# Split weights for the last eight column tiles of block 0 in a fused attention, feed-forward and expert kernel

## The chip, the cores and the metric

The kernel runs on one NeuronCore of a Trainium2 chip. The metric is the device time of one execution in microseconds (us). Three executions of the kernel before took 616.04, 618.12 and 615.83 us, median 616.04. The profile is of one execution that took 618.46 us; its traced span is 616.5 us, and 1.96 us lie around it.

## The reference

```python
scores = q @ k.T / sqrt(D)              # 2 batches, 8 heads, 768 positions, D = 64
keep   = (pos < 4) | (0 <= row - col < 128)   # 4 sink positions and a window of 128
a      = softmax(where(keep, scores, -1e9))
x      = (a @ v) as 1536 tokens x 512
h      = x @ w_in                       # 512 x 2048, given in float64
g      = maximum(0.01 * h, h)
x      = g @ w_out                      # 2048 x 512, given in float64
# then top-1 routing to 8 experts (512 -> 1024 -> 512, relu, capacity 384),
# each token's result times its gate probability
```

All results are float32. The two matrices of the first feed-forward network, `w_in` and `w_out`, arrive as float64 and are brought to float32 on the chip.

## The kernel before

The 1536 tokens are worked in six blocks of 256 (`j` = 0 to 5). For each block the first feed-forward network walks through its 2048 hidden columns in 16 tiles of 128 (`f`; `i` counts the iterations). For a tile, `FFN.first` (L841) multiplies the 512 inputs with the tile's columns of `w_in` into one PSUM bank `hps` of 128 x 256, `leak` applies the leaky ReLU, `split_g` splits the result in a high and a low part, and `second` (L887) multiplies it with the tile's rows of `w_out` and adds up into two PSUM banks `y`, 128 x 512 each. `second` runs `LAG` = 2 iterations behind `first`.

There are two ways to multiply. Blocks 1 to 5 use split operands: every float32 operand is the sum of a high part (rounded to float32r) and a low part (the rest, also float32r), and a product is three passes: high with high, high with low, low with high. The weights' parts are `wh` and `wl`, the inputs' `xth` and `xtl`, those of g the two halves of `gp`. Block 0 multiplies plain float32 operands, `cvt` (the converted weights) with `xth` (which holds float32 in block 0) and `gr`.

In block 0 the leaky ReLU is made of two ScalarE activations that both read `hps` (L852, L853) and a subtraction on GpSimd (L854). In the others it is a scaling on ScalarE (L857), a maximum on VectorE that reads `hps` and the scaled copy (L858), a cast on ScalarE (L867, high part) and a subtraction on GpSimd (L869, low part). While block 0 runs there is one bank for `hps`; later there are two.

Each tile's weights (512 KB as float64 in each matrix) are loaded by the SP queue, four tiles of buffers in all, and turned into float32 by VectorE: three instructions of 128 x 512 for each matrix (L779, L783, L789), so six for a tile. `convert()` runs four tiles ahead of `first` and is over with iteration 11 of block 0. `split` (L809, L810) makes `wh` by a cast on ScalarE and `wl` by a subtraction, on GpSimd in block 0 and on VectorE in block 1. A matrix of a tile is queued for splitting when its second product in block 0 is issued; one is split in each iteration of block 0 from the third on (14 of 32), two in each of block 1. Tiles 0, 1, 14 and 15 are also stored to a scratch in HBM (`wscr`, L814), since only 14 tiles' parts are kept, and reloaded later.

Between the steps of a block lie the steps of the attention for the tokens of the next block: 20 of them during block 0. An attention unit has, among others, `sps` (L501, scores), copies and predicated copies on ScalarE and VectorE (L506, L513), the maximum of a row `mx` (L514), exponentials (L219), the reciprocal of the sum `ri` (L226, L227), the scaling on GpSimd (L229), transposes, and the product with v (`ops`, L568).

Nearly all tiles of SBUF, converted weights, parts of weights, g, and the attention's keys, queries, values and transposed parts, come from one pool `c` of 70 buffers of 2 KB a partition. A buffer is given back after the last use of what it holds, and whoever asks for one when none is free waits.

The instructions of TensorE, ScalarE, GpSimd and of the SP queue keep the order in which the program is written. VectorE's order is made by a planner ahead of the run, by priority; the conversions in the loop over the blocks stand 100 behind (`BEHIND`). Every engine executes its queue in order. The clears of the result's buffers (`places<-zero`) are issued on the SP queue from iteration 8 on, two an iteration.

Of the kernel before, what the change touches and what calls it, by code (L numbers as in the profile page):

```python
# [8 lines left out]
F32 = mybir.dt.float32  # L9
F32R = mybir.dt.float32r  # L10
# [3 lines left out]
ALU = mybir.AluOpType  # L14
# [4 lines left out]
P = 128  # L19
# [19 lines left out]
LAG = 2  # L39
SPLIT = (1, 2)  # L40
CLEAR_AT, CLEAR = 8, 2
ROUTE = (2, 5, 9, 10, 11, 14)
HOLD, TAIL = 4, 1
QUIET = 2
# [676 lines left out]
class FFN:  # L721
# [12 lines left out]
    def __init__(self, nc, pools, A, xt, cap):  # L734
        self.nc, self.p, self.A = nc, pools, A
        self.xt, self.CAP = xt, cap
        self.DM, self.DFF = A["shape_in"]
        self.K = self.DM // P
        self.NF = self.DFF // P
        self.wide = A["w_wide"]  # L740
        self.w, self.v, self.raw, self.g, self.y = {}, {}, {}, {}, {}
        n = max(0, self.NF - self.CAP)
        self.saved = set(range(n)) | set(range(self.NF - n, self.NF))
        self.scr = self.p["dram"].tile([self.NF, 4, P, 512], F32, name="wscr") if n else None
# [58 lines left out]
    def split(self, f, x, eng):  # L803
# [8 lines left out]
        if f in self.saved:  # L812
            for a, t in enumerate((h, l)):
                nc.sync.dma_start(out=self.scr[f, 2 * x + a], in_=t.bitcast(F32))  # L814

    def reload(self, f):
        nc, c = self.nc, self.p["c"]
        self.w[f] = {}
        for x in range(2):
            t = [c.tile([P, 512], F32R, tag="c", name=nm) for nm in ("wh", "wl")]  # L820
            for a in range(2):
                nc.sync.dma_start(out=t[a].bitcast(F32), in_=self.scr[f, 2 * x + a])
            self.w[f][x] = t
# [5 lines left out]
    def first(self, j, f):  # L829
        nc, N = self.nc, self.N  # L830
        ps = self.p["psh"].tile([P, 512], F32, tag="h", name="hps")[:, 0:N]
        kc = lambda t: t.rearrange("p (k c) -> p k c", k=self.K)
        if j:
            wh, wl = map(kc, self.w[f][0])
            xh, xl = self.xt(j)
            mm = ((wh, xh), (wh, xl), (wl, xh))
        else:
            mm = ((kc(self.v[f][0]), self.xt(j)[0]),)
        mm = [(w[:, k, :], x[:, k, :]) for k in range(self.K) for w, x in mm]
        for n, (w, x) in enumerate(mm):  # L840
            nc.tensor.matmul(ps, lhsT=w, rhs=x, start=(n == 0), stop=(n == len(mm) - 1))  # L841
        self.g[j, f] = ps

    def leak(self, j, f):

        nc, N = self.nc, self.N
        ps = self.g[j, f]
        if j == 0:

            t = self.p["c"].tile([P, 2, N], F32, tag="c", name="gr")  # L850
            g, r = t[:, 0], t[:, 1]
            nc.scalar.activation(g, ps, AF.Relu)  # L852
            nc.scalar.activation(r, ps, AF.Relu, scale=-0.01)  # L853
            nc.gpsimd.tensor_tensor(out=g, in0=g, in1=r, op=ALU.subtract)  # L854
        else:
            g = self.p["g"].tile([P, N], F32, tag="g", name="g")
            nc.scalar.activation(g, ps, AF.Copy, scale=0.01)  # L857
            nc.vector.tensor_tensor(out=g, in0=ps, in1=g, op=ALU.max)  # L858
        self.g[j, f] = g

    def split_g(self, j, f, end=False):
        nc, N = self.nc, self.N
        g = self.g[j, f]
        if j == 0:
            return
        gp = self.p["c"].tile([P, 2, N], F32R, tag="c", name="gp")
        nc.scalar.copy(gp[:, 0], g)  # L867
        eng = nc.vector if end else nc.gpsimd
        eng.tensor_tensor(out=gp[:, 1], in0=g, in1=gp[:, 0].bitcast(F32), op=ALU.subtract)  # L869
        self.g[j, f] = gp  # L870

    def second(self, j, f, start, stop, tiles):
        nc = self.nc
        gp = self.g[j, f]
        if start:
            self.y[j] = [self.p["psy"].tile([P, self.DM], F32, tag=f"y{t}", name=f"y{t}")
                         for t in range(self.N // P)]
        for t in tiles:
            y = self.y[j][t]
            sl = slice(t * P, (t + 1) * P)  # L880
            if j:
                wh, wl = self.w[f][1]
                mm = ((gp[:, 0, sl], wh), (gp[:, 0, sl], wl), (gp[:, 1, sl], wh))
            else:
                mm = ((gp[:, sl], self.v[f][1]),)
            for n, (l, r) in enumerate(mm):
                nc.tensor.matmul(y, lhsT=l, rhs=r, start=(start and n == 0), stop=(stop and n == len(mm) - 1))  # L887
# [696 lines left out]
def build(tc, A, n_sink, window, capacity):  # L1584
    nc = tc.nc
# [3 lines left out]
    ring = RingAttention.fits(n_sink, window)  # L1589
# [9 lines left out]
    with ExitStack() as es:  # L1599
# [63 lines left out]
        ffn = FFN(nc, p, A, xt, FFN.CAP if ring else FFN.CAP - FEWER // 4)  # L1663
# [14 lines left out]
        def some(calls, n):  # L1678
            for f in calls[:n]:
                f()  # L1680
            del calls[:n]
# [19 lines left out]
        nclear = CLEAR * (ffn.NF - CLEAR_AT)  # L1701
        rate = -(-max(0, rt.NU * rt.E - nclear) // ROUTE[3])
        ex = Experts(nc, tc, p, A, rt, ident)
# [3 lines left out]
        pending, held, routing, splits = [], [], [], []  # L1707
# [7 lines left out]
        def split(n, f=-1, x=0):  # L1715

            while splits and (n > 0 or f >= 0 and x not in ffn.w.get(f, ())):
                ffn.split(*splits.pop(0), nc.vector if j else nc.gpsimd)
                n -= 1

        def second():
            j, f, i = pending.pop(0)
            if j == 1:
                split(0, f, 1)
            last = i == ffn.NF - 1
            if j == late and i >= ffn.NF - HOLD:

                ffn.second(j, f, i == 0, last, range(TPB - 1))
                held.append((j, f, i))
                if last:  # L1730
                    for t in range(TPB - 1):
                        rt.evac(j * TPB + t, ffn.y[j][t])
                return
            ffn.second(j, f, i == 0, last, range(TPB))
            del ffn.g[j, f]
            if j == 0:
                splits.extend((f, x) for x in range(2))
            elif i < n_ev or j == late:
                del ffn.w[f]
            if j > 1 and i < n_ev:  # L1740
                ffn.reload(ffn.order(j)[ffn.CAP + i])
            if last:
                ts = tuple(range(j * TPB, (j + 1) * TPB))
                for t, y in zip(ts, ffn.y.pop(j)):
                    rt.evac(t, y)
                routing.extend(route(ts))
                if j == late - 2 and rt.NU:
                    routing.insert(-1, ex.rank)

        for j in range(NB):  # L1750
# [9 lines left out]
            for i, f in enumerate(ffn.order(j)):  # L1760
# [18 lines left out]
                    step()  # L1779
                    ndone += 1  # L1780
                some(conv, 99)
                split(SPLIT[min(j, 1)])
                if j > 0 or i >= CLEAR_AT:
                    some(clears, max(1, rate) if j else CLEAR)
                if routing and i in ROUTE:
                    routing.pop(0)()
# [91 lines left out]
```

## Time and profile before

| | |
|---|---|
| median of three executions | 616.04 us (615.83 to 618.12) |
| profiled execution | 618.46 us, span 616.5 us |
| granted clock of TensorE | 0.984 of full speed in the mean |
| TensorE matmul busy | 586.6 us, 95% of the span, 3889 instructions |
| VectorE busy | 382.7 us, 62%, 928 instructions |
| ScalarE busy | 311.9 us, 51%, 920 instructions |
| GpSimd busy | 179.2 us, 29%, 328 instructions |
| moved by DMA | 91.88 MB, 149 GB/s in the mean |

Block 0 lasts from about 37 to 122 us, blocks 1 to 5 to about 431 us; the experts follow. A busy share is an average over all of these. In a row PE is TensorE, PEld its weight load, DVE VectorE, ACT ScalarE, POOL GpSimd and SP the queue that issues most DMAs. `L841` is line 841 of the kernel; `out<-in` names the tiles written and read. A time in brackets is idle time ahead of an instruction and what ended it. The chain of waits follows the last instruction back through whatever released it, so it tells at every time which engine the end hangs on.

### The profile page before, as it was taken

The page shows a single profiled execution, that of the slowest core. Times are in us where ns is not written, and L with a number is a line of the kernel's source. Part 1 is how long each engine was busy: PE and PEld are TensorE (multiplying, and loading weights), DVE is VectorE, ACT ScalarE, POOL GpSimd, SP SyncE. Part 2 cuts the span into 40 slices and gives each one's busy share as a digit, 9 for nine tenths or more (in the row PEclk, how much of TensorE's full clock was granted, in tenths as well). Part 3 has the DMA queues.
Part 4 walks back from the last instruction along what each step waited for, and adds up shares of the span by engine and source line. Part 5 has one row for each costly group of instructions (what it writes and reads, how often), then busy time and mean ns, then how long its engine had stood idle before and what let it go on. Part 6 is the DMA issues. An engine that isn't in the chain of part 4 may idle for free.

```text
span 616.5 us, 11665 instructions
## 1 busy us (share of the span) xinstructions
PE 586.6 (95%) x3889; PEld 502.4 (81%) x3889; DVE 382.7 (62%) x928; ACT 311.9 (51%) x920; POOL 179.2 (29%) x328
## 2 busy tenths in 40 slices
PE   7698998999999999999999999999999999999994
PEld 7575665689889888998889988988798989998783
DVE  4789998377854555555655542266456676655992
ACT  4665555576655455545555433254244544444772
POOL 4425555633342224332422232223110120102110
PEclk9899999999999999999999999999969999999998
DMA  9769989622653402330223015755165856643950
GB/s 244 185 206 249 294 231 269 158 83 53 226 185 108 115 19 69 87 103 19 61 58 98 1 48 164 259 183 165 59 207 172 259 177 204 195 133 111 304 188 12
DMA packets 83564, 91.88 MB, mean 149 GB/s; under 512 B 42964, under 2 KB 51156, under 8 KB 83473
## 3 DMA queue, kind: packets, MB, share of 16 engines
q1 hardware_dynamic: 81488, 85.68, 47.1%
q0 software_dynamic: 1984, 5.13, 2.3%
q8 instruction: 39, 0.64, 0.4%
q14 instruction: 53, 0.43, 0.2%
HBM read 72.01 MB, written 20.09 MB: 149 GB/s over the span
## 4 chain that ended last, share of the span: by engine, by line
PE 70%; DVE 13%; DMA 7%; issue 7%; ACT 3%; POOL 0%; another core or an unknown queue 0%; POOLq 0%; SPq 0%; ACTq 0%; DVEq 0%
PE y L887 18%; PE hps L841 17%; PE ph L1306 10%; PE py L1355 8%; PE ops L568 4%; DVE cvt L789 3%; PE sps L501 3%; DMA out<-ys,gt 2%; DVE word L779 2%; DVE word L783 2%; DMA craw<-in_moe_w 2%; PE lps L972 2%; PE sps L652 1%; PE pps L536 1%; PE kps L163 1%
## 5 line engine op out<-in xcount | busy, mean ns | idle before, releaser
L887 PE MATMUL y<-wh,gp 128*128 128x512 f32 x320 | 115.9, 403 | 0.7 <-ACT gp L867 0.7
L869 POOL TENSOR_TENSOR gp<-g,gp 128x256 fp32r<-128x256 f32 x77 | 56.8, 738 | 197.3 <-ACT gp L867 172.3
L841 PE MATMUL hps<-xth,wh 128*128 128x256 f32 x320 | 92.8, 290 | 0.0
L841 PE MATMUL hps<-xtl,wh 128*128 128x256 f32 x320 | 90.1, 281 | 0.0
L841 PE MATMUL hps<-xth,wl 128*128 128x256 f32 x320 | 89.9, 281 | 0.0
L1170 DVE TENSOR_TENSOR cw<-craw,cw 128x512 fp32r<-128x512 f32 x128 | 83.4, 695 | 9.1 <-ACT cw L1168 7.9
L1168 ACT CAST cw<-craw 128x512 fp32r<-128x512 f32 x112 | 63.4, 621 | 23.7 <-PE py L1355 22.3
L887 PEld LDWEIGHTS y<-wh,gp 128*128 128x128 f32 x320 | 60.0, 188 | 14.3 <-issue 2.7
L857 ACT ACTIVATE g<-hps 128x256 f32<-128x256 f32 x80 | 30.6, 382 | 70.0 <-PE hps L841 65.7
L1355 PE MATMUL py<-cw,ht 128*128 128x512 f32 x264 | 63.9, 397 | 0.2 <-DVE ht L1343 0.2
L841 PEld LDWEIGHTS hps<-xth,wh 128*128 128x128 f32 x320 | 60.3, 188 | 3.3 <-issue 0.9
L841 PEld LDWEIGHTS hps<-xtl,wh 128*128 128x128 f32 x320 | 60.3, 188 | 3.1 <-issue 0.7
L887 PE MATMUL y<-wl,gp 128*128 128x512 f32 x160 | 62.7, 392 | 0.0
L1306 PE MATMUL ph<-xt,cw 128*128 128x256 f32 (+2 forms) x444 | 62.3, 304 | 0.4 <-issue 0.4
L1306 PEld LDWEIGHTS ph<-xt,cw 128*128 128x128 f32 x444 | 61.1, 204 | 0.7 <-issue 0.5
L841 PEld LDWEIGHTS hps<-xth,wl 128*128 128x128 f32 x320 | 60.6, 189 | 0.0
L1355 PEld LDWEIGHTS py<-cw,ht 128*128 128x128 f32 x264 | 49.1, 189 | 11.5 <-DVE ht L1343 0.7
L858 DVE TENSOR_TENSOR g<-hps,g 128x256 f32<-128x256 f32 x80 | 33.4, 418 | 25.6 <-ACT g L857 25.3
L219 ACT ACTIVATE pm<-pm,mx 128x132 f32<-128x132 f32 (+1 forms) x80 | 31.7, 398 | 29.1 <-DVE mx L514 28.9
L867 ACT CAST gp<-g 128x256 fp32r<-128x256 f32 x80 | 33.3, 416 | 23.8 <-DVE g L858 23.6
L1364 POOL DMA_INDIRECT out<-ys,gt x11 | 11.4, 1036 | 114.7 <-DVE ys L1363 114.7
L543 DVE TENSOR_TENSOR pt<-pps,both 128x512 f32<-128x512 f32 x28 | 19.3, 688 | 35.7 <-PE pps L538 35.7
(211 smaller groups left out, 1121.0 us busy)
## 6 DMA issues: line engine op xcount, KB each, us to landing
craw<-in_moe_w SPq DMA_DIRECT2D x128, 256.0 KB, 3.5
rawi<-in_moe_w_in SPq DMA_DIRECT2D x16, 512.0 KB, 5.0
rawo<-in_moe_w_out SPq DMA_DIRECT2D x16, 512.0 KB, 5.4
places<-zero SPq DMA_DIRECT2D x24, 257.0 KB, 5.7
wh<-wscr SPq DMA_DIRECT2D x16, 256.0 KB, 2.9
wl<-wscr SPq DMA_DIRECT2D x16, 256.0 KB, 3.4
xg<-places SPq DMA_DIRECT2D x12, 257.0 KB, 4.4
natv<-in_v SPq DMA_DIRECT2D x12, 256.0 KB, 5.2
```

The costliest lines, as they stand in the source:

```text
L219: nc.scalar.activation(pm[:, e, 0:w], pm[:, e, 0:w], AF.Exp, bias=mx[:, e:e + 1], accum_out=su[:, e:e + 1])
L568: nc.tensor.matmul(ps[64 * e:64 * e + 64, :], lhsT=l, rhs=r, start=(x == 0), stop=(x == len(mm[0]) - 1))
L841: nc.tensor.matmul(ps, lhsT=w, rhs=x, start=(n == 0), stop=(n == len(mm) - 1))
L857: nc.scalar.activation(g, ps, AF.Copy, scale=0.01)
L858: nc.vector.tensor_tensor(out=g, in0=ps, in1=g, op=ALU.max)
L867: nc.scalar.copy(gp[:, 0], g)
L869: eng.tensor_tensor(out=gp[:, 1], in0=g, in1=gp[:, 0].bitcast(F32), op=ALU.subtract)
L887: nc.tensor.matmul(y, lhsT=l, rhs=r, start=(start and n == 0), stop=(stop and n == len(mm) - 1))
L1168: nc.scalar.copy(h, t)
L1170: eng.tensor_tensor(out=l, in0=t, in1=h.bitcast(F32), op=ALU.subtract)
L1306: nc.tensor.matmul(self.ph[f][:, sl], lhsT=self.w[e, "a", h, k][w][:, f * P:(f + 1) * P], rhs=self.xt[:, a, k, sl], start=(m == 0), stop=( ...
L1355: nc.tensor.matmul(self.py[n], lhsT=x, rhs=w, start=(h == 0 and f == 0 and m == 0), stop=(h == self.NH - 1 and f == self.HF - 1 and m == 2))
```

## The change

The products of the last eight column tiles of block 0 (f = 8 to 15) use split operands, as the blocks after it do. For this the inputs of block 0 are split once, in iteration 5 (`split_x0`: two casts on ScalarE and two subtractions on GpSimd, 128 x 512, into four buffers of the pool `c`). In iterations 6 to 13 both matrices of the tile two ahead are split on GpSimd in place of the one from the queue; these tiles go the way of the later blocks in `leak`, `split_g` and `second`, and aren't queued for splitting any more. The rule for the second way is `in_parts`, asked in `first`, `leak`, `split_g` and `second` (the line with `if j == 0:` below stands so in both `leak` and `split_g`). In the remaining iterations the queue is served as before, so 6 of the first eight tiles' 16 matrices are split in block 0 and 10 in block 1.

```diff
+AHEAD = 8
...
+    def split_x0(self):
+        nc, c = self.nc, self.p["c"]
+        for k in range(0, self.K, 2):
+            x = self.xt(0)[0][:, k:k + 2, :]
+            h, l = (c.tile([P, 2, self.N], F32R, tag="c", name=nm) for nm in ("x0h", "x0l"))
+            nc.scalar.copy(h, x)
+            nc.gpsimd.tensor_tensor(out=l, in0=x, in1=h.bitcast(F32), op=ALU.subtract)
+            self.x0.append((h, l))
+
+    def in_parts(self, j, f):
+        return j > 0 or f in self.ahead
...
-        if j:
+        if self.in_parts(j, f):
             wh, wl = map(kc, self.w[f][0])
-            xh, xl = self.xt(j)
+            xh, xl = [[x[:, k, :] for k in range(self.K)] for x in self.xt(j)] if j else \
+                [[self.x0[k // 2][a][:, k % 2, :] for k in range(self.K)] for a in range(2)]
             mm = ((wh, xh), (wh, xl), (wl, xh))
...
-        if j == 0:
+        if not self.in_parts(j, f):
...
-            if j:
+            if self.in_parts(j, f):
...
-                splits.extend((f, x) for x in range(2))
+                splits.extend((f, x) for x in range(0 if f in ffn.ahead else 2))
...
-                split(SPLIT[min(j, 1)])
+                if j == 0 and ring and i == AHEAD - 3:
+                    ffn.split_x0()
+                if j == 0 and ring and AHEAD <= i + 2 < ffn.NF:
+                    ffn.ahead.add(i + 2)
+                    for x in range(2):
+                        ffn.split(i + 2, x, nc.gpsimd)
+                else:
+                    split(SPLIT[min(j, 1)])
```

## Rows read from the trace of the kernel before

**Rows 1.** The page's chain that ended last, shares of the span by line.
```profile
PE y L887 18%; PE hps L841 17%; PE ph L1306 10%; PE py L1355 8%; PE ops L568 4%; DVE cvt L789 3%; PE sps L501 3%; DMA out<-ys,gt 2%; DVE word L779 2%; DVE word L783 2%; DMA craw<-in_moe_w 2%; PE lps L972 2%; PE sps L652 1%; PE pps L536 1%; PE kps L163 1%
```
**Rows 2.** Busy by stretch (us): stretch, length, PE, PEld, DVE, ACT, POOL, clock, DMA.
```profile
85.50:107.00 21.50, 19.48 (x106) 13.51 (x107) 18.45 (x41) 13.30 (x45) 10.62 (x16) 1.00 1.04 259
107.00:122.00 15.00, 15.00 (x80) 9.84 (x79) 6.43 (x17) 9.09 (x30) 9.22 (x15) 1.00 0.71 174
122.00:134.00 12.00, 12.00 (x78) 9.32 (x77) 6.87 (x17) 7.23 (x22) 5.12 (x9) 1.00 0.36 110
```
**Rows 3.** The chain in order of time: start us, us, what.
```profile
107.03 1.72 PE y L887 x4
...
108.75 1.73 PE hps L841 x8
...
113.20 1.73 PE hps L841 x8
...
122.58 1.43 PE hps L841 x12
...
132.91 1.39 PE y L887 x6
```
**Rows 4.** Timeline of VectorE, 74 to 124 us: start us, us, instruction, [idle before].
```profile
101.41 0.49 DVE L513 COPY_PREDICATED pm<-sel,sps 128x128 f32<-128x128 int32 x2
...
103.83 0.17 DVE L226 TENSOR_SCALAR ri<-su 128x2 f32<-128x2 f32 x1 [1.01 <-ACT pm L219]
...
106.37 0.69 DVE L789 SCALAR_TENSOR_TENSOR cvt<-rawo,word 128x512 int32<-128x512 int32 x1
```
**Rows 5.** Timeline of TensorE, 78 to 108 us.
```profile
78.65 1.89 PE L841 MATMUL hps<-xth,cvt 128*128 128x256 f32 x8
...
98.42 1.88 PE L887 MATMUL y<-cvt,gr 128*128 128x512 f32 x4
...
101.75 0.54 PE L197 MATMUL qps<-ident_r,qs 128*128 128x128 f32 x4 [0.18 <-DVE pm L513]
...
102.13 1.96 PE L841 MATMUL hps<-xth,cvt 128*128 128x256 f32 x8
...
106.40 0.64 PE L501 MATMUL sps<-kT,qT 128*128 128x264 f32 x3 [1.04 <-DVE qT L202]
```
**Rows 6.** Groups by line and shape: xcount | busy us, mean ns | idle before.
```profile
L857 ACT ACTIVATE g<-hps 128x256 f32<-128x256 f32 x80 | 30.6, 382 | 70.0 <-PE hps L841 65.7 <-PE y L887 1.8 <-PE pps L538 1.5
...
L858 DVE TENSOR_TENSOR g<-hps,g 128x256 f32<-128x256 f32 x80 | 33.4, 418 | 25.6 <-ACT g L857 25.3
...
L854 POOL TENSOR_TENSOR gr<-gr 128x256 f32<-128x256 f32 x16 | 11.9, 743 | 14.3 <-ACT gr L853 14.2
...
L810 POOL TENSOR_TENSOR wl<-cvt,wh 128x512 fp32r<-128x512 f32 x14 | 18.4, 1314 | 28.9 <-ACT wh L809 28.9
...
L809 ACT CAST wh<-cvt 128x512 fp32r<-128x512 f32 x32 | 19.5, 641 | 0.0
```
**Rows 7.** Waits between 78 and 107 us: in total, times, longest.
```profile
ACT pm L219 <- DVE mx L514: 8.6, 3, 4.5
```
**Rows 8.** Timeline of GpSimd, 60 to 135 us.
```profile
78.00 1.45 POOL L810 TENSOR_TENSOR wl<-cvt,wh 128x512 fp32r<-128x512 f32 x1
```
**Rows 9.** Timeline of VectorE, the operation ri.
```profile
78.25 1.23 DVE L226 TENSOR_SCALAR ri<-su 128x2 f32<-128x2 f32 x1
...
87.62 0.17 DVE L226 TENSOR_SCALAR ri<-su 128x2 f32<-128x2 f32 x1 [1.01 <-ACT pm L219]
```
**Rows 10.** Timeline of the SP queue.
```profile
103.78 0.39 SPq L140 DMA_DIRECT2D natk<-in_k  x1
...
121.74 0.39 SPq L140 DMA_DIRECT2D natv<-in_v  x1
```
**Rows 11.** Timeline of ScalarE, 122 to 136 us.
```profile
126.93 0.43 ACT L149 CAST ks<-natk 128x256 fp32r<-128x256 f32 x1
```
**Rows 12.** Waits of the SP queue, 96 to 150 us.
```profile
SPq L140 <- PE y L887: 19.0, 1, 19.0
```

More of the change, by code (lines that the diff above doesn't have):

```diff
@@ L741, in __init__ @@
         self.w, self.v, self.raw, self.g, self.y = {}, {}, {}, {}, {}
+        self.ahead, self.x0 = set(), []
         n = max(0, self.NF - self.CAP)
@@ L832, in first @@
         kc = lambda t: t.rearrange("p (k c) -> p k c", k=self.K)
-        if j:
+        if self.in_parts(j, f):
             wh, wl = map(kc, self.w[f][0])
-            xh, xl = self.xt(j)
+            xh, xl = [[x[:, k, :] for k in range(self.K)] for x in self.xt(j)] if j else \
+                [[self.x0[k // 2][a][:, k % 2, :] for k in range(self.K)] for a in range(2)]
             mm = ((wh, xh), (wh, xl), (wl, xh))
         else:
-            mm = ((kc(self.v[f][0]), self.xt(j)[0]),)
-        mm = [(w[:, k, :], x[:, k, :]) for k in range(self.K) for w, x in mm]
+            x = self.xt(j)[0]
+            mm = ((kc(self.v[f][0]), [x[:, k, :] for k in range(self.K)]),)
+        mm = [(w[:, k, :], x[k]) for k in range(self.K) for w, x in mm]
         for n, (w, x) in enumerate(mm):
@@ L863, in split_g @@
         g = self.g[j, f]
-        if j == 0:
+        if not self.in_parts(j, f):
             return
```

## The prediction

> **What bounds the kernel now.** I read the page's busy shares and chain first, then the chain in order of time through block 0, then the engines' busy time by stretch, then each engine's timeline where the chain changes hands.
>
> TensorE's products of the first feed-forward network, L887 and L841, head the chain that ended last; of VectorE's lines there the conversion of the weights has three (L789, L779, L783, 3 + 2 + 2%) [rows 1]. That conversion happens only up to the end of block 0, so the question is which engine carries block 0 when its last eight tiles run. The stretches answer it [rows 2]. Between 85.5 and 107 us VectorE is busy 18.45 of 21.50 us and TensorE 19.48; between 107 and 134 us TensorE is busy 27.00 of 27.00 and VectorE 13.30. In order of time the chain is VectorE's conversions and the attention work between them, then softmax and copies on ScalarE and two copies of qT on VectorE, and from 106.4 TensorE alone, product after product without a break [rows 3]. VectorE's timeline shows the hand-over: two predicated copies at 101.41 stand behind a conversion, and the last conversion begins at 106.37 [rows 4]. TensorE's timeline agrees: it waits for those copies at 101.75 (0.18 us) and last for VectorE's qT at 106.40 (1.04 us) [rows 5].
>
> Tiles 8 to 12, five, have their first product from 78.65 to 102.13, and the second product of tile 9, the latest ahead of the hand-over, is at 98.42 [rows 5]. So tiles 8 to 12 with their first product, and 8 and 9 with their second, run while VectorE is the bound. The first products of tiles 13 to 15 and the second ones of 10 to 15 lie in TensorE's own stretch.
>
> **The change part by part.**
>
> *The products.* In block 0 a first product is eight records in 1.73 us and a second one four in 1.72; in block 1, with split operands, they are twelve in 1.43 and six in 1.39 [rows 3]. A tile saves 0.30 + 0.33 = 0.63 us. Behind 107 us that is 3 x 0.30 + 6 x 0.33 = 2.9 us, all on the path, since TensorE has no gap there. Ahead of 107 us it is 5 x 0.30 + 2 x 0.33 = 2.2 us, which I count as nothing: TensorE would reach the copies at 101.41 sooner and wait. Its bounds are 0 and -2.2.
> [...]
>
> *The leaky ReLU of the eight tiles.* Before, two ScalarE reads of the product (0.38 each, as the scaling's) and a GpSimd subtraction (0.74); after, one ScalarE scaling (0.38), a VectorE maximum (0.418), a ScalarE cast of the same size and a GpSimd subtraction of the same shape [rows 6]. ScalarE and GpSimd come out even. VectorE gains 0.418 us a tile. Tiles 8 to 11 come ahead of its last conversion: 4 x 0.418 = 1.67 us on the bound; the other four lie where VectorE is half idle and cost nothing. Bounds: 0, if they fall into gaps such as that of 1.01 us at 103.83 [rows 4]; and 1.67 + 4 x 0.32 = 2.9, if each maximum also holds VectorE up until ScalarE's scaling is done, as the 25.6 us of idle time over 80 of them say [rows 6]. I take 1.67.
> There is one bank for the first product in block 0, so the next first product waits for the last reader. That was ScalarE's second read; now it is VectorE's maximum, behind at most one conversion (0.68 to 0.70, as the one at 106.37 [rows 4]): 0.38 + 0.70 + 0.42 = 1.50 us after the product. A second product (1.39) and mostly attention stand between: at most 0.1 us a tile. Nothing.
>
> *The weights split two tiles ahead.* Eight more splits move from VectorE in block 1 to GpSimd in block 0, a second one in each of the iterations 6 to 13. ScalarE casts earlier, not more in all: eight times 0.64 us, and two more casts for x; it is busy 13.30 of 21.50 and 9.09 of 15.00 us [rows 2, 6], and its own waits for VectorE's maxima of the scores (8.6 us between 78 and 107) cover it [rows 7]. Without that cover it is up to 10 x 0.64 = 6.4 us; I take 0. GpSimd takes ten more subtractions of 1.31 us [rows 6]. Until 107 it has room, 10.62 of 21.50 us busy. From 107 to 122 it is busy 9.22 of 15.00 [rows 2], 2.7 us of each interval of 4.4 (108.75 to 113.20 [rows 3]); with a second subtraction that is 4.0 against 4.4 - 0.6 = 3.8. In iterations 12 and 13 it falls behind by 0.2 us each, and two tiles of lead hold that. 0; the other end is both subtractions in full, 2.6. Block 1 gives nothing back: TensorE is busy all of 122 to 134 us, so 5.5 us less of VectorE there (8 x 0.69, its size in block 1 by estimate from the 0.68 to 0.70 of a conversion of the same shape [rows 4]) is off the path.
>
> *GpSimd against VectorE.* The tiny scaling ri (128x2) takes 0.17 us alone at 87.62, and 1.23 us at 78.25, just behind the start of a wl at 78.00 on GpSimd [rows 8, 9]. A hit costs 1.06 us, and until 107 on the bound. There are four ri from 78 to 107 us, one an attention unit. With two subtractions in a row instead of one I take one hit more, 1.06 us. Bounds: 0 and three more, 3.2. The maximum itself is not held up so: its mean over 80 is 418 ns [rows 6], beside GpSimd's subtractions of g.
>
> *Queues and space.* The scratch stores of tiles 14 and 15 (eight of 256 KB) come forward from block 1 to iterations 12 and 13. Behind them on the SP queue wait the clears, which nothing needs soon, and the keys issued at 103.78 [rows 10] with their queries; ScalarE takes those keys at 126.93 [rows 11]. Issued after the split of tile 15 (about 112 to 115 us by the intervals above), they have over 10 us to land. 0; the other end is a tile's interval, 4.4. The pool of 70 buffers holds, by the code, 14 x 2 + 18 = 46 weights at the end of block 0 now and 22 x 2 + 10 = 54 then, plus four for x until tile 15. The load of v issued at 121.74 already waits for a buffer that a second product frees, 19.0 us [rows 10, 12]. Extra waits there are free; on ScalarE's queue one would not be (below).
>
> *Sum:* -2.9 + 1.67 + 1.06 = -0.2 us. The profiled execution took 618.46 us (616.5 of span); so 618.3 for it, and on the median of 616.04, **615.9 us**. No change that can be told: what TensorE saves behind 107 us is about what VectorE loses ahead of it.
>
> **The rivals.**
> 1. *VectorE's additions find gaps and TensorE keeps everything.* For it: TensorE is busy 19.48 of the 21.50 us from 85.5 [rows 2], so it is nearly a bound itself, and VectorE has 3 us idle between 85.5 and 107. Against: the chain there runs through VectorE without a break, and its order is fixed before the run. 8 x 0.63 = 5.0: 611.0 us.
> 2. *GpSimd holds VectorE off (slower).* Place: ri and the small operations of attention on VectorE, iterations 6 to 11; price 1.06 each. -2.9 + 1.67 + 1.06n passes +3.1 from n = 5 on: 620.1. For it: ri is hit already with half the subtractions [rows 8, 9]. Against: the maxima and the conversions, most of the work there, show no such lengths [rows 4, 6].
> [...]
> 3. *ScalarE waits for a buffer (slower).* With 54 + 4 weights and x, three of g and a dozen of attention the pool is full from iteration 13 to block 1's second. ScalarE is in order; a cast that waits for a second product to free its buffer waits up to a tile's interval, 4.4 us. Against: blocks 1 and later run full without such a wait. -0.2 + 4.4: 620.2.
> 4. *The saving doesn't arrive,* since TensorE waits for GpSimd's wl or low part of g: the 2.6 us above, 618.5.
>
> **How the numbers follow.** 0.5% is 3.1 us, about what a measurement of this kernel can tell from no change. The forecast with its own range (613.0 to 618.2: one end with the maxima and hits free, the other with the larger price of the maxima and two hits): 0.52. Rival 1: 0.20. Rivals 2 and 3: 0.10 each. Rival 4: 0.08. Faster: rival 1 and a little of the forecast, 0.23; slower: rivals 2 and 3, 0.20; same 0.57. The range reaches from 611.5, near rival 1, to 620.0, near rivals 2 and 3.
>
> **What would show it.** Right: first products of tiles 8 to 15 as twelve records in about 1.43 us; eight more wl on GpSimd (22 in all), ten on VectorE; VectorE's last conversion about 2.7 us later than 107.1; TensorE's gaps ahead of it grown by 4 to 5 us; behind it no gap; block 1's first product at about 121.8 instead of 122.0, and everything after it shifted by that. Wrong: the last conversion at 107 or before (rival 1); ri above 1 us five times or more (rival 2); ScalarE's or TensorE's idle time near 115 to 130 us ended by a release of a buffer (rival 3); weight loads of the first product that wait for wl (rival 4).

## The result: slower by 3.4 us

The changed kernel took 619.99 us in the median (618.10 to 621.34), the kernel before beside it 616.58 (615.83 to 618.12): ratio 1.0054, 95% interval 1.0038 to 1.0069. Forecast were 615.9 us and no change that can be told; the range reached to 620.0. Run again in a later batch, the same code took 622.78 against 617.49 (1.0100, 1.0076 to 1.0123). Times of one kernel spread by 2 to 9 us from execution to execution (two that took more than twice as long, 1492.67 us of the maximum alone and 1434.94 of a kernel before, are in no ratio). A profile is of one execution: that of after took 620.08 us (span 618.3, mean granted clock 0.987), that of before 618.46 (616.5, 0.984). The latter is longer than each of the eight that its median of 616.58 comes from, so the two profiles lie closer together than the medians.

All 17 profiles of this study (the two given ones, one of after again, 14 of variants) can be cut into the same stages: what lies ahead of block 0's first product, block 0 from there to the first transposition `xps` of its result (some 12 us into block 1), blocks 1 to 5 up to the last `xps`, and the experts behind. The first stage takes 35.7 to 37.0 us (52.9 in one variant), blocks 1 to 5 take 298.2 to 298.7 us in every profile. So a loss of several us lies in block 0 or behind block 5. In the two profiles of after, block 0 took 98.56 and 97.58, and 97.09 in that of before; behind block 5 it is 184.3 and 184.4 against 183.9.

Inside block 0 the terms are not those of the prediction. By stretches after (length, TensorE, its weight loads, VectorE, ScalarE, GpSimd, clock, DMA), to be set against [rows 2]:
```profile
85.50:107.00 21.50, 17.62 (x133) 13.97 (x133) 18.50 (x42) 12.98 (x42) 13.43 (x19) 1.00 0.86 231
107.00:122.00 15.00, 12.45 (x90) 10.13 (x91) 8.42 (x20) 11.23 (x35) 12.91 (x17) 1.00 0.54 195
```
GpSimd went from 10.62 and 9.22 us to 13.43 and 12.91. TensorE idles 3.9 us in the first stretch and 2.6 in the second, where it idled 2.0 and not at all; VectorE is as full as before in the first stretch and fuller in the second. TensorE's timeline (start, us, instruction, idle time before it and its releaser) names the new waits:
```profile
77.08 0.80 PE L569 MATMUL ops<-pt,natv 128*64 128x128 f32 x8 [1.88 <-POOL pt L551]
...
98.53 0.38 PE L858 MATMUL hps<-x0h,wh 128*128 128x256 f32 x1 [2.55 <-DVE g L875]
```
The product with v (`ops`) waits five times, 5.1 us in all, for masks that GpSimd lays over `pt` (L551), and the first product of tile 11 waits once for VectorE's maximum that frees the single bank. None of them is in the kernel before. GpSimd's timeline ahead of the first one:
```profile
71.64 2.51 POOL L825 TENSOR_TENSOR x0l<-xth,x0h 128x512 fp32r<-128x512 f32 x2 [6.53 <-ACT x0h L824]
74.10 1.29 POOL L812 TENSOR_TENSOR wl<-cvt,wh 128x512 fp32r<-128x512 f32 x1
75.33 0.65 POOL L230 TENSOR_TENSOR pm<-pm,ri 128x264 f32<-128x264 f32 x1
75.92 0.75 POOL L871 TENSOR_TENSOR gr<-gr 128x256 f32<-128x256 f32 x1
76.60 0.79 POOL L551 TENSOR_SCALAR_AFFINE_SELECT pt<-pt 128x256 f32<-128x256 f32 x2
```
GpSimd stands idle for 6.53 us, then has 5 us of work ahead of the mask. It waits for ScalarE's cast of x, which stands in ScalarE's timeline behind exponentials that wait for VectorE's row maximum:
```profile
68.55 0.41 ACT L220 ACTIVATE pm<-pm,mx 128x132 f32<-128x132 f32 x1 [4.52 <-DVE mx L515]
...
70.92 1.16 ACT L824 CAST x0h<-xth 128x512 fp32r<-128x512 f32 x2
```
The split is written behind the iteration's second attention step, so two in-order queues pass that wait on.

### The profile page after: what moved, and what is told of

Read it like the earlier page. It is cut to its first block, busy times and chain, and to the rows that moved or that the text cites. A ratio compares the mean times of both kernels' runs of the same rounds, so it can differ in the third digit from the quotient of the medians.

```text
span 618.3 us, 11785 instructions
## 1 busy us (share of the span) xinstructions
PE 579.5 (94%) x3937; PEld 501.1 (81%) x3937; DVE 383.2 (62%) x928; ACT 314.3 (51%) x922; POOL 189.4 (31%) x338
## 5 line engine op out<-in xcount | busy, mean ns | idle before, releaser
L904 PE MATMUL y<-wh,gp 128*128 128x512 f32 x352 | 127.6, 403 | 0.7 <-ACT gp L884 0.7
L886 POOL TENSOR_TENSOR gp<-g,gp 128x256 fp32r<-128x256 f32 x85 | 63.4, 746 | 198.5 <-ACT gp L884 172.5
L904 PEld LDWEIGHTS y<-wh,gp 128*128 128x128 f32 x352 | 66.1, 188 | 15.8 <-issue 3.3
L874 ACT ACTIVATE g<-hps 128x256 f32<-128x256 f32 x88 | 33.6, 382 | 76.2 <-PE hps L858 75.6
L904 PE MATMUL y<-wl,gp 128*128 128x512 f32 x176 | 69.0, 392 | 0.0
L1323 PE MATMUL ph<-xt,cw 128*128 128x256 f32 (+2 forms) x444 | 59.2, 295 | 1.1 <-DVE xt L1311 1.1
L1323 PEld LDWEIGHTS ph<-xt,cw 128*128 128x128 f32 x444 | 58.0, 194 | 1.4 <-DVE xt L1311 1.3
L875 DVE TENSOR_TENSOR g<-hps,g 128x256 f32<-128x256 f32 x88 | 36.8, 418 | 28.4 <-ACT g L874 28.1
L884 ACT CAST gp<-g 128x256 fp32r<-128x256 f32 x88 | 36.6, 416 | 31.1 <-DVE g L875 29.8
```

The costliest lines, as they stand in the source:

```text
L1323: nc.tensor.matmul(self.ph[f][:, sl], lhsT=self.w[e, "a", h, k][w][:, f * P:(f + 1) * P], rhs=self.xt[:, a, k, sl], start=(m == 0), stop=( ...
```

## Experiments on block 0

**Load alone.** The kernel before with ten subtractions more on GpSimd, which read what was long there:
```diff
+        def load(t):
+            spare = p["c"].tile([P, 2, N], F32, tag="c", name="spare")
+            nc.gpsimd.tensor_tensor(out=spare, in0=t, in1=t, op=ALU.subtract)
...
+                if j == 0 and i == AHEAD - 3:
+                    for k in range(0, ffn.K, 2):
+                        load(xt(0)[0][:, k:k + 2, :])
+                if j == 0 and AHEAD <= i + 2 < ffn.NF:
+                    load(ffn.v[i + 2][0].rearrange("p (k c) -> p k c", k=2))
```


> The kernel before, with ten more GpSimd subtractions of 128x512 at the places where the change puts its ten (two in iteration 5 on the inputs, one in each of iterations 6 to 13 on weights); their results are used by nothing. Measure: time from block 0's first product to the first transpose of its result (97.1 us before, 98.6 after the change) and the total. Theory G (GpSimd's queue holds up the masks pt that TensorE's ops wait for, and the small operations of VectorE): TensorE waits for pt 3 to 5 us in all, block 0 is 2 to 4 us longer, total +2 to +4 us. Theory V (VectorE's maximum holds the only bank of the first product): no change, within 0.5 us in block 0, total within 1 us.


617.29 us, ratio 0.9989 (0.9974 to 1.0004); block 0 97.92, as in other kernels with an unchanged block 0 (below), and one wait of `ops` for a mask, 0.63 us. GpSimd's load by itself costs nothing that shows.

**The maximum alone.** Tiles 8 to 15 of the kernel before with the scaling, VectorE's maximum from the bank and one addition of zero on GpSimd:
```diff
+            if f >= AHEAD:
+                nc.scalar.activation(r, ps, AF.Copy, scale=0.01)
+                nc.vector.tensor_tensor(out=r, in0=ps, in1=r, op=ALU.max)
...
+                nc.gpsimd.tensor_tensor(out=g, in0=r, in1=self.zero, op=ALU.add)
```


> The kernel before, plain products, but tiles 8 to 15 of block 0 make g by a ScalarE scaling, a VectorE maximum that reads the bank, and one GpSimd addition of zero in place of the subtraction (same shape, so GpSimd's load stays). Theory V: TensorE waits for the maximum about 2.5 us around tile 11, VectorE's last conversion is 1.7 us or more later, block 0 is 1.5 to 3 us longer, total +1.5 to +3 us. Theory G: no wait above 0.5 us, block 0 within 0.7 us of 97.1, total within 1 us.


619.89 us, 1.0028 (1.0009 to 1.0046); block 0 98.15. Neither theory has it: the total is near theory V's, but the bank didn't hold TensorE. At 84.19 `ops` waited 3.08 us for GpSimd's masks, which stood behind the addition that waited for a late maximum.

**The bank freed by ScalarE.** The changed kernel with two activations of ScalarE in block 0 and VectorE's subtraction in SBUF:
```diff
+            if j == 0:
...
+                nc.scalar.activation(g, ps, AF.Relu)
+                nc.scalar.activation(r, ps, AF.Relu, scale=-0.01)
+                nc.vector.tensor_tensor(out=g, in0=g, in1=r, op=ALU.subtract)
```


> The changed kernel, but the bank is read by ScalarE alone: two activations as in the kernel before, then a VectorE subtraction of the two in SBUF in place of the maximum. Theory V: the wait of 2.55 us ahead of tile 11's first product goes, block 0 falls from 98.6 to about 96.2 us, total -2.4 against the changed kernel, so about +1 against the kernel before. Theory G: another wait takes its place, above all for pt; block 0 stays within 0.7 us of 98.6, total +2.5 to +4.


624.76 us, 1.0105 (1.0070 to 1.0140); block 0 102.33. The wait of 2.55 us is gone, but the waits for masks grow to 3.87 and 2.83 us. The maximum as the cause of the loss falls.

**The splits sooner.** The changed kernel with the casts and subtractions ahead of the second attention step:
```diff
+                if early_split(j, i):
+                    if i == AHEAD - 3:
+                        ffn.split_x0()
...
                 while more():
                     step()
...
-                if j == 0 and ring and i == AHEAD - 3:
-                    ffn.split_x0()
```


> The changed kernel, but the splits of the tile two ahead (and of the inputs) stand ahead of an iteration's second attention step instead of behind it, so ScalarE casts and GpSimd subtracts while ScalarE would wait for VectorE's row maxima. Theory G: TensorE's waits for pt (5.1 us in five gaps) fall below 2 us, block 0 falls from 98.6 to 95 to 97 us, total -1.5 to -3.5 against the changed kernel, so about 0 against the kernel before. Theory V: the wait for the maximum stays at about 2.5 us and block 0 within 0.7 us of 98.6.


Block 0 95.35, as expected, and one wait for a mask is left (0.83 us at 98.41). So the order of the queues was what cost there. But the whole took 619.18 us, 1.0024 (1.0002 to 1.0046): the stage behind block 5 was 190.1 us long where it is 183.9 in the profile of before. A stage that no edit had touched was 6 us longer, in a profile whose execution is the longest of the twelve (622.69 us).

## Experiments behind block 5

**Four runs to see whether that is chance, a shift, or code.** The changed kernel again; sooner splits with the leak of block 0 as before (`if j == 0:` in `leak`); the kernel before with 40 short products in place of 10 at its start; and with the last tile's first products of block 0 computed twice:
```diff
-WARM = 10
+WARM = 40
...
-            nc.tensor.matmul(warm, lhsT=ident, rhs=ident, start=True, stop=True)
+            nc.tensor.matmul(warm[:, 0:16], lhsT=ident, rhs=ident[:, 0:16], start=True, stop=True)
...
+        for again in range(2 if j == 0 and f == 15 else 1):
```


> The changed kernel once more, beside the others of this batch, for a second trace of it. Theory Q (GpSimd's in-order queue: masks stand behind subtractions that wait for ScalarE's casts) expects block 0 (first hps to first xps) at 98.3 to 98.8 us again, with five waits of TensorE's ops for the masks that sum to 4.5 to 5.5 us. On the whole time 1.003 to 1.007 of before.


Block 0 97.58, shorter than expected, and the same five waits; 622.78 us, 1.0100, a larger loss than expected.


> The changed kernel with the splits ahead of the second attention step, and in block 0 the leak as before (two activations of ScalarE, a subtraction of GpSimd) instead of VectorE's maximum. Theory Q and the experiment with sooner splits leave in block 0: one wait of 0.3 us for the maximum and the work of eight maxima on VectorE. If VectorE's maxima cost only themselves (1.67 us of its work), block 0 comes to 94.0 to 95.3 us, 0 to 1.3 under the 95.35 of sooner splits. Rival: GpSimd, which then has eight subtractions more (3.2 us), is the queue that fills, and waits of ops for masks come back: block 0 at 96 to 97.5. Whole time by the first 614 to 617, by the rival 617 to 620.


Block 0 96.71, as the rival has it, and waits for masks are back (2.12 and 1.75 us); 619.01 us, 1.0026 (0.9997 to 1.0055). The stage behind block 5 is long again, 185.5 us.


> The kernel before, with 40 products of 16 columns in place of the 10 of 128 columns that stand at the start of TensorE's queue: some 60 matmul records more ahead of everything, as the change has 48 more, and no other work. Theory I (the expert stage behind block 5 grows because the instructions of its branches lie at other places) expects 1 to 2 us behind the last transposition of block 5 and 618.3 to 619.5 in all. Theory N (the stage's length only spreads from execution to execution, and the change loses there by chance) and theory T (it grows because it is reached later) expect no change: 617 to 618.


635.17 us, 1.0280 (1.0256 to 1.0304). It failed as a probe: a float32 record of 16 columns took 0.216 us, nearly the 0.227 of one of 128, so that all came 16 us later. The stage behind block 5 took 187.3 us.


> The kernel before, with the first products of block 0's last column tile computed twice (the second overwrites the first): 1.7 us more of TensorE at the end of block 0, at almost the same number of instructions. Theory T (the expert stage grows because it is reached later, so that its transfers fall at other times) expects 2.7 to 3.7 us in all: 1.7 in block 0 and 1 to 2 behind block 5. Theories I and N expect 1.7 in block 0 and nothing behind: 1.2 to 2.2 in all.


620.48 us, 1.0062 (1.0037 to 1.0087): 3.0 us for 1.7 us of products, theory T's number. But the edit also adds eight records, and TensorE stops for 2.20 us near 72 us behind block 5; this run can't tell whether the shift or the records did that.

The profiles show something else. Behind block 5 GpSimd issues two scatters of the routing; the second waits for the landing of the first (it starts 0.80 to 0.81 us behind it in all 17 profiles), and the experts' first transposition `px` waits for a load `xg` behind both. In all profiles the first scatter starts 4.5 us behind block 5. The second follows 3.5 to 4.0 us later in some kernels and 4.3 to 5.2 us in others, and in the latter a packet of an instruction queue (8 or 14) moves beside the scatter's. In the kernel before, queue 8 carries 39 packets and 0.64 MB, 16.4 KB each; in blocks 1 to 5 one comes every 117 to 149 product records of TensorE, with a mean near 128, and with the 48 records that the change adds the one behind block 5 comes 11 us sooner. So I take queue 8 for TensorE's code.

**Code alone.** Three kernels with short float32r products (2 columns) ahead of waits of TensorE before 29 us, 10 + 16 + 22 = 48 in the kernel before and 8 + 11 + 15 = 34 in the change with and without sooner splits:
```diff
+FILL = (10, 16, 22)
...
+        w = self.ident_r[:, 0:out.shape[0]]
+        for _ in range(n):
+            self.nc.tensor.matmul(out[:, 0:2], lhsT=w, rhs=self.ident_r[:, 0:2], start=True, stop=True)
```


> The kernel before with 48 short float32r products (2 columns) ahead of waits of TensorE between 11 and 28 us: as many more as the change adds, and no other work. In the traces so far TensorE's instruction stream is loaded by queue 8, and of two scatters of the routing the second starts 8.1 to 8.4 us behind the last transposition of block 5 in four kernels with the old or nearly the old number of products and 9.2 to 9.7 us in the five with 48 more, in which a packet of queue 8 lies between the two scatters. Theory I (that packet delays the landing of the first scatter, and the expert stage pays) expects the packet there, the second scatter at 9.1 to 9.5, the wait of px for xg at 1.9 to 2.2 us, and 618.5 to 620.5 in all against 617.5. Theory N (the two have nothing to do with each other) expects 8.1 to 8.4 and 617 to 618.

> The changed kernel with 34 short float32r products at the same places. By theory I the packet moves ahead of the first scatter (the packets have moved earlier by 11 us for 96 instructions), the second scatter goes back to 8.1 to 8.5 and the wait of px to 0.7 to 1.4 us: 618 to 620 in all where the changed kernel took 620.0 and 622.8. By theory N it stays at 620 to 623, or gets longer by what the short products cost.

> The changed kernel with the splits ahead of the second attention step, and the same 34 short products. That order won about 2.7 us of block 0 against the usual 98 of the kernel before, and lost it again behind block 5 (190.1 us against 183.9). By theory I the second scatter goes back to 8.1 to 8.5, and the whole comes to 614.5 to 617, under the kernel before. By theory N it stays at 618 to 620.


The kernel before with 48 took 619.84 us, 1.0050 (1.0027 to 1.0073): products that compute nothing new, hidden in waits, cost 2.4 us in the medians (1.7 to 4.5 by the interval), where the change costs 3.4 and 5.3. The packet came where expected, but the second scatter did not move (3.87 us behind the first), so theory I was right on the time and wrong on the way. Its profiled execution took 618.15, near the lowest of its twelve (617.92 to 624.45), and doesn't show where the median loses.
The other two contradict its times: 625.46 (1.0128, 1.0096 to 1.0159) and 623.93 (1.0118, 1.0100 to 1.0136), 2.7 to 5.5 us more than without the short products, although the packet of queue 8 moved ahead of the scatter as expected. Their profiles show a new stop. TensorE's timeline and stretches of the first (columns as above):
```profile
479.24 0.49 PE L1318 MATMUL ph<-ident,xg 128*128 128x128 f32 x3
483.77 0.47 PE L1318 MATMUL ph<-ident,xg 128*128 128x128 f32 x1 [4.04 <-issue]
```
```profile
480.00:485.00 5.00, 1.23 (x6) 1.23 (x7) 0.25 (x1) 0.67 (x2) 1.28 (x3) 0.81 0.40 136
485.00:490.00 5.00, 5.00 (x24) 5.00 (x25) 3.34 (x6) 2.38 (x5) 0.00 (x0) 0.50 0.47 150
490.00:495.00 5.00, 5.00 (x32) 5.00 (x31) 1.03 (x3) 0.77 (x2) 0.00 (x0) 0.67 0.67 221
```
Between the third and the fourth of four like products TensorE stops for 4.04 us and waits for nothing that the profile shows ("issue"). DMA between 480 and 484 us:
```profile
q14 instruction: 3, 0.02, 1.9%
q8 instruction: 1, 0.02, 1.5%
```
A packet of queue 8, by the above TensorE's code, comes in just there, and behind the stop the granted clock is 0.50 from 485 to 490 us and 0.67 in the mean of the next 5 us. The second kernel has 3.31 us at the same place, the kernel before nothing, though a packet of queue 8 comes in 48 us behind block 5 there too; so the packet by itself is not the stop. In blocks 1 to 5 of the kernel before, some 128 records, each a weight load and a product, go with a packet of 16.4 KB (the packets of queue 14 are half as long, 8.2 KB); the expert stage is the one with branches at run time, and in the kernel before, packets come there after 5 to 118 records instead of 117 to 149. No run here took a branch away, so the branch as the cause of the stops is not shown.

**A whole packet.** If the place in the packet decides, 48 + 80 = 128 records put everything behind block 0 back where it was:
```diff
+FILL = (18, 28, 34)
```


> The changed kernel with 80 short float32r products ahead of waits of TensorE before 29 us: with the change's 48 that is 128 records, and the packets of queue 8 lie 117 to 148 records apart in the long stretches (0.64 MB in 39 packets). Theory I2 (TensorE's instructions come in packets of some 128 products, and the jumps of the expert stage cost what their place in a packet makes of it) expects the packets where they lie in the kernel before (4 to 6 us ahead of the last transposition, 16 to 18 and 34 us behind it), no wait near 49 us, one of 0.4 to 1.3 us near 74, and 616.5 to 618.5 in all: the change's loss is gone, its block 0 neither gains nor loses. Theory M (every product more costs, wherever it stands) expects over 625, since 34 took it to 625.5.

> The changed kernel with the splits ahead of the second attention step and the same 80 short products. By theory I2 block 0 takes 95 to 96 us as before in this order, the expert stage what it takes in the kernel before, and the whole 614 to 616: the first version under the kernel before. By theory M over 623.


The changed kernel with 80 idle products more: 616.78 us, 0.9998 (0.9983 to 1.0013), 3.2 to 6.0 us less than without them. Theory M, a price per product, falls: the cost goes with the place of the code, not with the number of products. The stop that the 34 products brought near 49 us is not there, nor the changed kernel's near 72, and `px` waits 0.72 us:
```profile
439.21 1.00 POOL L1063 DMA_INDIRECT places<-x,rsi  x1 [8.33 <-DVE rs L1039]
442.81 0.97 POOL L1063 DMA_INDIRECT places<-x,rsi  x1 [2.60 <-DVE again L1113]
448.60 0.63 PE L1318 MATMUL px<-ident,xg 128*128 128x128 f32 x4 [0.72 <-DMA xg<-places]
```
Theory T, the time at which the stage is reached, falls too: with 34 and with 80 products the changed kernel is behind block 5 at the same 434.7 us, and needs 190.8 and 180.3 us from there. But the stage isn't just back where it was: 180.3 us is 3.6 less than in the profile of before, and makes up for a block 0 that took 99.48. The kernel before with 128 idle products, which would have to take its own time again, was not run.

The sooner splits with 80: 616.83, 0.9988 (0.9970 to 1.0006), 0.8 us above what was expected; block 0 95.42, but still 4.72 us between the scatters, 2.08 us of wait at `px` and the clock down behind it. A packet of queue 14 lay with the scatter's; up to here it was there in the kernels whose traces have 1171 to 1175 rows of VectorE (all that it executes, waits and branches included), and not in those with 1164 to 1168.

**That packet taken away, and put in.** The old leak with sooner splits and 80; and the changed kernel with 80 and eight small instructions more on VectorE at the start:
```diff
-                    nc.vector.memset(k[64 - 64 * e:128 - 64 * e, e], 0.0)
+                    for pr in range(2):
+                        nc.vector.memset(k[64 - 64 * e:128 - 64 * e, e, pr], 0.0)
```


> Splits ahead of the second attention step, the leak of block 0 as before, and 80 short products. So far the second scatter starts 8.0 to 8.4 us behind block 5 where no instruction packet (queue 8 or 14) lies with the first scatter's packets 6.0 to 6.8 us behind it, and 8.8 to 9.7 where one does; with 80 short products more and sooner splits one of queue 14 still does. In the kernels with 2255 or 2256 instructions of VectorE there is none of queue 14, in those with 2259 to 2263 there is. Theory P (a packet there delays the landing by 0.8 to 1.3 us, TensorE waits that much longer for xg, and its clock falls behind the longer wait) expects, at 2255 and with queue 8 moved a whole packet, none in that place: second scatter 8.0 to 8.5, the wait of px at 0.7 to 1.4, block 0 at 96 to 97 and 614.5 to 616.5 in all. Theory R (the longer wait comes with the order of the sooner splits) expects the scatter at 9.2, px at 2.1, and 616.5 to 618.5.

> The changed kernel with 80 short products, and the eight clearings of the key tiles at the start in two halves each: eight instructions of VectorE more (2264 for 2256), about the same work. Theory P expects a packet of queue 14 with the first scatter's packets, the second scatter at 8.8 to 9.7 instead of 8.0, the wait of px at 1.4 to 2.2 instead of 0.72, and 0.7 to 5 us in all behind the 616.8 without them, the more the clock falls. Theory R expects 8.0 to 8.4, 0.7 to 1.4 and 616 to 617.5.


Both are as theory P has it for the packet and the scatters. Eight small clearings more, 430 us ahead, cost 3.3 us between the medians (2.4 by the ratios): 620.04, 1.0037 (1.0018 to 1.0057). DMA of the first scatter in that kernel, and its scatters and `px`:
```profile
q0 software_dynamic: 80, 0.15, 13.8%
q14 instruction: 1, 0.01, 1.1%
issues: line engine op xcount, KB each, median us to landing
places<-x,rsi POOLq DMA_INDIRECT x1, 3.5
```
```profile
437.51 1.00 POOL L1064 DMA_INDIRECT places<-x,rsi  x1 [8.35 <-DVE rs L1040]
441.85 0.97 POOL L1064 DMA_INDIRECT places<-x,rsi  x1 [3.34 <-ACT hs L1365]
448.06 0.63 PE L1319 MATMUL px<-ident,xg 128*128 128x128 f32 x4 [1.88 <-DMA xg<-places]
```
Without the packet the same scatter landed in 2.8 us. The old leak with 80 has no packet there, 3.85 us between the scatters (1.55 us at `px`, a little over expectation), block 0 of 95.74 (a little under), and takes 616.10 us against 617.98: 0.9965 (0.9946 to 0.9984), the first version that beats both kernels, by 1.9 us between the medians.

All profiles, in us:

| kernel | block 0 | behind block 5 | between scatters, packet with the first | wait at `px` | TensorE's longest wait 45 to 75 us behind block 5 |
|---|---|---|---|---|---|
| before | 97.09 | 183.9 | 3.87, none | 1.25 | 0.41 |
| after | 98.56 | 184.3 | 4.69, queue 8 | 2.03 | 1.47 |
| after again | 97.58 | 184.4 | 4.86, queue 8 | 2.00 | 1.51 |
| load alone | 97.92 | 183.9 | 3.54, none | 1.04 | 1.22 |
| maximum alone | 98.15 | 183.8 | 4.28, queue 14 | 1.40 | 1.04 |
| bank freed | 102.33 | 185.6 | 5.00, both | 2.19 | 1.15 |
| splits sooner | 95.35 | 190.1 | 5.21, both | 2.54 | 1.69 |
| old leak, sooner | 96.71 | 185.5 | 4.68, queue 8 | 2.09 | 1.2 |
| short at start | 98.10 | 187.3 | 3.83, none | 1.20 | 1.34 |
| late by 1.7 | 99.79 | 184.4 | 3.62, none | 0.74 | 2.20 |
| before, 48 short | 98.30 | 183.6 | 3.87, queue 8 just behind | 1.42 | 1.12 |
| after, 34 short | 99.34 | 190.8 | 3.95, none | 1.46 | 4.04 |
| sooner, 34 short | 95.36 | 189.6 | 4.72, queue 14 | 1.76 | 3.31 |
| after, 80 short | 99.48 | 180.3 | 3.60, none | 0.72 | under 0.25 |
| sooner, 80 short | 95.42 | 185.6 | 4.72, queue 14 | 2.08 | 0.47 |
| old leak, 80 short | 95.74 | 184.3 | 3.85, none | 1.55 | under 0.25 |
| after, 80 short, 8 vector | 98.67 | 185.1 | 4.34, queue 14 | 1.88 | 0.28 |

TensorE's clock hides part of this in single profiles. From block 5 to TensorE's last product it is 166.6 to 168.0 us in all 17, plus two things: the time that TensorE idles (3.6 us before, 6.5 and 6.6 after, 6.0 with the 48 idle products, 8.5 in both with 34, 3.7 to 4.5 in the four with 80) and, by estimate, half of the time that the clock stood at 0.50 (5.1 us lost so before, 1.7 in both of after, none in after with 80, 8.5 in splits sooner). So 2.9 us more idle time after stand against 3.4 us less lost to the clock, and the two profiles look alike behind block 5. But idle time doesn't follow TensorE's code alone: load alone and maximum alone, with no product more, have 6.1 and 5.8 us.

## Why the prediction was wrong

**The step that failed** is "Queues and space ... 0", with its end, "everything after it shifted by that". The prediction went through the SP queue, ScalarE's queue and the pool of buffers, and left out queues 8 and 14, whose packets the profile lists as instructions. By estimate the change's 48 more product records move the code of the expert stage by three eighths of a packet (48 of some 128 records). 48 idle products in the kernel before have a price of that size, 2.4 us (1.7 to 4.5) against 3.4 and 5.3, and 80 more in the changed kernel, which make 128 with them, take the loss away (0.9998), though its block 0 stays as long as it was. How one execution's loss divides between the wait for `xg`, the stops of TensorE and the clock behind them differs from profile to profile, and for the median execution it stays open.

A second term at 0 failed inside block 0: "The weights split two tiles ahead", of which the prediction counted only busy time. It took ScalarE's waits for VectorE's row maxima as cover for the casts; the casts stood behind those waits, and GpSimd's masks behind the casts. Written behind the attention step they cost 3.3 us of block 0 against the same splits ahead of it (98.7 against 95.4 in the mean, below).

**The products:** the mechanism was right, the size nearly. The twelve records of a first product follow each other 0.12 us apart (104.91 to 106.29 for tile 12), as in block 1. From TensorE's last wait for qT (106.40 before, 108.79 after) to `xps` pass 27.7 us before and 26.6 after; without the new wait of 1.06 us at 119.68 that is 2.2 us less, where 2.9 were forecast. (In three other profiles with block 0 unchanged it is 29.4, the clock at 0.50 for some 3 us of it.) Block 1's first product came at 124.23 and 123.24. The 121.8 us forecast for it counted in the second products of tiles 14 and 15, which come behind it, so by the prediction's own terms it was 122.5.

**The maxima:** the shift came out, by luck. The last conversion of VectorE's timeline,
```profile
108.77 0.69 DVE L791 SCALAR_TENSOR_TENSOR cvt<-rawo,word 128x512 int32<-128x512 int32 x1
```
began at 106.37 before [rows 4]; counted from block 0's start it is 2.6 us later (predicted 2.7, with the hit). But with the same maxima and the splits sooner it begins 69.1 to 69.5 us behind block 0's start in three profiles, where the kernel before has 69.3 and the change's own order 70.9 to 72.9 in five. So most of the 2.6 us is again the place of the splits; taking the maxima off VectorE in the sooner order gained 0.6 us there, and 1.7 with 80 idle products. "At most 0.1 us a tile. Nothing" for the single bank was wrong once, 2.55 us at tile 11: ahead of the maximum stood `ks` in 1.51 us, `qs`, `ri` and a conversion.

**The splits on GpSimd** are as many as forecast (groups: count | busy us, mean ns | idle before):
```profile
L812 POOL TENSOR_TENSOR wl<-cvt,wh 128x512 fp32r<-128x512 f32 x22 | 28.5, 1311 | 16.4 <-ACT wh L811 16.4
...
L812 DVE TENSOR_TENSOR wl<-cvt,wh 128x512 fp32r<-128x512 f32 x10 | 7.0, 725 | 2.0 <-ACT wh L811 1.8
```
"Until 107 it has room" was true of busy time and wrong of the queue. A second subtraction costs nothing that shows by its length, as the load alone has it, but where it waits for ScalarE, the masks behind it wait too. Placed ahead of the attention step it costs little: block 0 takes 95.35 to 95.42 us in three profiles so, against a mean of 98.7 in the five with the change's own order, and of 97.9 in four where block 0 isn't touched (97.09, 98.10, 98.30, and 99.79 less 1.73). So block 0 is 0.8 us longer, not 0.2 shorter; such profiles spread by 1 to 2 us, so that the 0.8 is rough.

**GpSimd against VectorE:** right in number. From 67 to 107 us two instructions of VectorE are long, one more than before, though neither is `ri`:
```profile
77.39 1.52 DVE L183 SCALAR_TENSOR_TENSOR qs<-natq,qs 128x256 fp32r<-128x256 f32 x1
...
95.63 1.51 DVE L155 TENSOR_TENSOR ks<-natk,ks 128x256 fp32r<-128x256 f32 x1
...
112.89 1.25 DVE L227 TENSOR_SCALAR ri<-su 128x2 f32<-128x2 f32 x1
```
`ks` takes 0.43 us at 111.67, and 1.51 beside two `wl` that run from 94.34 to 96.86; the `ri` is behind the conversions and off the path.

**The rivals:** 1 fell with the late conversion, 2 with one long `ri` instead of five (two long instructions in all up to 107 us), 3 with no more than 0.8 us of ScalarE (`gp`) waiting for a `wl` of GpSimd. 4 was near in its form, GpSimd holding TensorE off, but by the masks and not by `wl`, and the loss goes away with 80 idle products while those waits stay.

## What to carry to other kernels

Here 48 product records more brought the packet of queue 8 behind block 5 11 us sooner, eight small instructions more on VectorE put a packet of queue 14 beside a scatter 430 us later, and 48, 82 and 128 records more, the change's own 48 included, had different prices (1.0054 and 1.0100, 1.0128, 0.9998). So before a gain or a loss is put down to a change that adds or takes away instructions, compare against a control with as many idle instructions, better several. Ahead of that, follow what is queued behind a new instruction for each in-order engine and what that instruction itself waits for; free busy time said nothing of it here: GpSimd stood idle for 6.53 us ahead of the work that held TensorE off for 1.88.

## What had not been expected of the hardware

With one packet of code, 8.2 or 16.4 KB, or one of each beside a scatter of 128 rows the next one came later: 4.28 to 5.21 us between them, and 3.54 to 3.95 without such a packet. The last of the scatter's 80 packets starts 6.8 us behind block 5 without it and 7.1 to 8.3 with it; in the one exception the packet came 0.14 us behind that last one. Behind waits of `px` from 1.04 to 2.54 us the granted clock lay below 1.00 in one to three stretches of 5 us; behind those of 0.72 and 0.74 us it stayed at 1.00. It isn't in proportion: 1.25 us before were followed by some 10 us at 0.50, 2.03 us after by some 3. And in the kernel before with 48 short products a float32r product of 2 columns took 0.12 us with 128 columns of weights and 0.065 with 64.
